# Eight of 24 chunk systems inverted whole on VectorE, and a later due time for K and Q loads

## The chip, the cores and the metric

One NeuronCore of a Trainium2 chip runs the whole program. The metric is the device time of one execution in microseconds; the time quoted is the median of the timed runs. Engines are named as in the profile: PE is TensorE (PEld its weight loads), DVE is VectorE, ACT is ScalarE, POOL is GpSimd, SP issues the DMAs.

## What is computed

A delta-rule attention layer (4 batches, 8 heads, 768 tokens, head size 48), followed by two feed-forward layers with 384 inputs and 2048 hidden units, all in float32.

```python
def _attn_ref(q, k, v, beta):
    k_n = k / (np.linalg.norm(k, axis=-1, keepdims=True) + 1e-06)
    state = np.zeros((B, H, D, D)); y = np.zeros_like(q)
    for t in range(S):
        kt, vt, bt = (k_n[:, :, t], v[:, :, t], beta[:, :, t, None])
        y[:, :, t] = np.einsum('bhd,bhde->bhe', q[:, :, t], state)
        v_old = np.einsum('bhde,bhd->bhe', state, kt)
        state = state + bt[:, :, :, None] * np.einsum('bhd,bhe->bhde', kt, vt - v_old)

h = x @ w_in;  g = np.maximum(h, 0.0) + np.log1p(np.exp(-np.abs(h)));  x = g @ w_out
h = x @ w2_in; g = h * np.cos(h);                                      out = g @ w2_out
```

## The kernel before

The 768 tokens are cut into 24 chunks of 32 (`C`), four chunks to a group (`NG` = 6 groups). Within a chunk the recurrence is a 32 x 32 unit lower triangular system for each batch and head. The kernel inverts its two 16 x 16 diagonal blocks ahead of time and couples them with matmuls in the step. All matmuls run on float16 pairs: a value is split in a high and a low part (`copy`, then a subtraction by `tt` or `stt`), and a product takes three passes (`HI_FIRST`), of which one pass over eight heads is eight matmuls of 48 columns.

The work of a group is in four parts:

- `norms(g)`: loads K of four chunks (`kt`), squares them on ScalarE into `sq`, reduces, takes reciprocal norms. For every group but the first it runs during the steps of the group before.
- `prep_k`, `prep_q`, `gram`: K is scaled, split, transposed, Q is loaded (`qt`) and split, both are stored (`kqd`) and loaded again as block-diagonal operands (`bdK`, `bdQ`, `bdA`); 40 matmuls of 64 columns give the gram of a chunk in `psA`. `take_A` copies its two diagonal blocks into `abuf` by an ACT copy and a DVE combination (with mask columns), and writes the coupling block `G` as a pair into the tail of `kp`; `take_P` makes the masked Q part; one DMA stores all of it (`kpd`).
- `solve(g)`: four chunks at once. DVE transposes `abuf` into `mlan`, so that each partition holds one system; it multiplies by beta and runs 15 pairs of multiply (`tmpd`) and subtract (`tlan`) for both blocks together. The result is split (`t16`), transposed into `tg`, stored in `tgd`.
- `step(n)`: `bt` from the state (matmuls with `bdK`), split to `b16`; a product with T (`bdT`, or `bdU`, which lies in the memory of `raw`) gives `u`; `u16` times the coupling block `bdG` corrects `bt`; split again; T product again; `u16` again; then the state, the output `y` and its transposed store to `xt`.

The first feed-forward layer runs in 12 blocks of two chunks (`moe_block(0, j)`: matmuls `psH<-xt,w` and `acc<-g,w` of 256 columns), the second in six blocks of 512 columns (`psH`, `psC`, `psY<-xu,v`). Weights are loaded as 64-bit words and converted on DVE, ACT and POOL (`conv`, tile `cv`). The second layer's weights take the memory of the whole preparation, which `open_wp2` frees after the last solve.

No order of the instructions is written by hand. `Plan` collects all operations with costs and dependences by keys, lays them out by a list schedule (six passes, priorities from a backward pass), and each engine then runs its queue in that order. A DMA counts as landed 0.9 us plus its `dma` and `slack` times after its issue; `slack` moves the users of a load later in the order, and the load earlier.

Of the kernel before, what the change touches and what calls it, by code (L numbers as in the profile page):

```python
# [52 lines left out]
N2 = C // 2  # L53
BOOST = 0.95
# [231 lines left out]
def delta_moe_moe_kernel(ctx, tc, q, k, v, beta, mask, w1, w2, out):  # L286
# [15 lines left out]
    mask_sb = const.tile([P, C + 3], F32, name="mask_sb")  # L302
# [36 lines left out]
    kpf = [pre.tile([P, 56 * C], F16, name=f"kp{i}") for i in range(4)]  # L339
    kpb = [x[:, 0:48 * C].rearrange("p (s h d l) -> p s h d l", s=3, h=H, l=2) for x in kpf]  # L340
    kgb = [x[:, 48 * C:].rearrange("p (h t l) -> p h t l", h=H, l=2) for x in kpf]
    kab = [pre.tile([P, H // 2, C, 2], F16, name=f"ka{i}") for i in range(2)]
    kqb = [pre.tile([P, 2, Z], F16, name=f"kq{i}") for i in range(4)]
# [3 lines left out]
    abuf = pre.tile([P, N2, 32], F32, name="abuf")  # L347
    mlan = pre.tile([P, N2, C], F32, name="mlan")
    tlan = pre.tile([P, N2, 2, N2], F32, name="tlan")
    t16 = pre.tile([P, C, C, 2], F16, name="t16")  # L350
    sq = pre.tile([P, H, D], F32, name="sq")
# [19 lines left out]
    kpd = dr.tile([NS, P, C * 56], F16, name="kpd")  # L371
    tgd = dr.tile([NG, P, 4, C * 16], F16, name="tgd")
    x2d = dr.tile([NB2, P, 2 * KC, 4 * P], F16, name="x2d")
# [105 lines left out]
    def norms(g):  # L479
        ss, n0, rn = nrm  # L480
        NK = [("n0",)]
        for n in range(4 * g, 4 * g + 4):
# [3 lines left out]
            dma(kt, k[n].rearrange("p (h d) -> p h d", h=H), kk, [("pre",)], 0.55, **A)  # L486
            if g:
                sqv, qk = sq, ("sq",)
# [3 lines left out]
            actf(sqv, kt, AF.Square, [qk], kk + [("pre",)], DM, **A)  # L492
# [43 lines left out]
    def prep_q(n):  # L536
# [3 lines left out]
        dma(qt, q[n].rearrange("p (s h t) -> p s h t", s=2, h=H), qk, [("pre",)], 0.73, **A)  # L540
        qv = kq[:, 1, 0:32 * C].rearrange("p (s h t l) -> p s h t l", s=2, t=C, l=2)
# [38 lines left out]
    def gram(n, bd, key, parts):  # L580
# [4 lines left out]
        mv = k_rows(n).unsqueeze(1) if n < 4 and s1 == 1 else kqb[s][:, s0:s1]  # L585
# [458 lines left out]
```

## Time and profile before

| | us |
|---|---|
| timed runs, median of 3 (lowest, highest) | 1045.03 (1044.27 to 1048.64) |
| profiled execution, its own time | 1038.81 |
| its span from first to last instruction | 1037.0 |
| TensorE busy | 940.1 (91%) |
| VectorE busy | 664.3 (64%) |
| ScalarE busy | 675.5 (65%) |
| mean granted clock of TensorE | 0.985 of full |

Busy time is a mean over stages: about 100 us of preparation and first steps, then 24 steps beside the first layer's blocks until about 660 us, then the second layer alone. Idle time of an engine is worth reading only where something behind it waits.

### The profile page before, as it was taken

Reading aid. Unit: us, or ns where it says so; the run is one execution under the profiler, and the core shown is the slowest. Engines: PE = TensorE matmul, PEld = TensorE weight load, DVE = VectorE, ACT = ScalarE, POOL = GpSimd, SP = SyncE. Lnnn points to the kernel's source line nnn. Section 1 sums busy time; section 2 is a strip of 40 time slices with the busy share of each in tenths; the row PEclk is TensorE's granted clock in tenths of the full one; section 3 lists DMA queues with packets and bytes.
Section 4 is the critical chain, followed back from the end, with each engine's and each line's share of the span. In section 5 each row is a group of like instructions: output and inputs, shape, how many; then the busy total and the mean of one; then the engine's idle time right before and its main releaser. Section 6 shows DMA issues by size and latency. Waiting matters only on the chain.

```text
span 1037.0 us, 27821 instructions
## 1 busy us (share of the span) xinstructions
PE 940.1 (91%) x11552; PEld 685.6 (66%) x11552; DVE 664.3 (64%) x1189; ACT 675.5 (65%) x1273; POOL 364.9 (35%) x331
## 2 busy tenths in 40 slices
PE   1135989989999999999999999999999999999998
PEld 1134878878898899899999997744444444444443
DVE  8999967457746854863575665686555555455454
ACT  5355858676777776866767887865555555554554
POOL 4012436333423442432332545553332223233232
PEclk9998989989999999999999999999999999999999
DMA  6998786877767775674558862101001010000000
GB/s 198 282 265 203 157 210 136 178 178 153 195 84 174 158 160 111 136 160 72 118 120 207 243 147 83 47 32 61 31 1 61 1 61 1 31 31 1 31 1 31
DMA packets 307741, 117.94 MB, mean 114 GB/s; under 512 B 272160, under 2 KB 287648, under 8 KB 307616
## 3 DMA queue, kind: packets, MB, share of 16 engines
q1 hardware_dynamic: 307616, 116.17, 46.4%
q8 instruction: 91, 1.49, 0.6%
q14 instruction: 34, 0.28, 0.1%
HBM read 71.03 MB, written 35.65 MB: 103 GB/s over the span
## 4 chain that ended last, share of the span: by engine, by line
PE 68%; DVE 11%; DMA 7%; ACT 7%; SPq 4%; issue 3%; POOL 1%; DVEq 0%; POOLq 0%; ACTq 0%
PE psH L812 19%; PE accA L874 14%; PE accB L874 10%; PE psC L812 7%; PE psA L874 6%; PE psC L691 5%; PE psY L812 4%; SPq L380 4%; PE psY L691 2%; DMA kt<-k_dram 2%; DMA kpd<-kp 2%; DMA qt<-q_dram 2%; DVE tmpd L401 1%; PE psA L597 1%; DVE cv L458 1%
## 5 line engine op out<-in xcount | busy, mean ns | idle before, releaser
L401 POOL TENSOR_TENSOR g<-g,g 128x512 f16<-128x512 f32 x191 | 227.4, 1191 | 464.9 <-ACT g L389 453.1
L812 PE MATMUL psH<-xt,w 128*128 128x256 f16 x1728 | 231.4, 275 | 3.3 <-DMA xt<-y 2.2
L389 ACT ACTIVATE g<-g 128x512 f16<-128x512 f32 x192 | 120.6, 629 | 100.2 <-DVE g L405 70.3
L874 PEld LDWEIGHTS <-w 128*128 128x128 f16 x1728 | 162.8, 98 | 24.8 <-issue 5.3
L812 PEld LDWEIGHTS <-w 128*128 128x128 f16 x1728 | 157.7, 98 | 22.1 <-DMA xt<-y 2.3
L874 PE MATMUL accA<-g,w 128*128 128x256 f16 x1152 | 159.9, 276 | 4.2 <-ACT g L389 2.8
L874 PEld LDWEIGHTS <-v 128*128 128x128 f16 x864 | 84.6, 98 | 101.9
L812 PEld LDWEIGHTS <-v 128*128 128x128 f16 x864 | 84.6, 98 | 100.9
L410 ACT ACTIVATE e<-e 128x512 f32<-128x512 f32 x96 | 60.4, 629 | 82.1 <-DVE e L405 82.0
L401 DVE TENSOR_TENSOR g<-psH,e 128x512 f32<-128x512 f32 x96 | 66.1, 688 | 55.9 <-ACT e L412 48.0
L874 PE MATMUL accB<-g,w 128*128 128x256 f16 x576 | 94.6, 273 | 0.3 <-POOL g L401 0.2
L812 PE MATMUL psH<-xu,v 128*128 128x512 f16 x351 | 83.1, 379 | 0.0
L812 PE MATMUL psC<-xu,v 128*128 128x512 f16 x342 | 81.5, 379 | 0.0
L874 PE MATMUL accB<-g,v 128*128 128x512 f16 x288 | 77.8, 379 | 0.0
L874 PE MATMUL accA<-g,v 128*128 128x512 f16 x288 | 77.8, 379 | 0.0
L874 PE MATMUL psA<-g,v 128*128 128x512 f16 x288 | 77.7, 379 | 0.0
L691 PEld LDWEIGHTS <-bdKQ 128*128 128x128 f16 x1840 | 65.1, 98 | 12.7 <-issue 10.6
L829 ACT ACTIVATE e<-psH 128x512 f32<-128x512 f32 x96 | 56.6, 590 | 22.6 <-PE psH L812 22.0
L412 ACT ACTIVATE e<-e,hpi 128x512 f32<-128x512 f32 x96 | 69.2, 721 | 3.0
L691 PEld LDWEIGHTS <-bdA 128*128 128x128 f16 x1680 | 56.1, 98 | 15.2 <-issue 13.0
L412 ACT ACTIVATE e<-e 128x512 f32<-128x512 f32 x96 | 60.0, 625 | 1.2
L835 ACT ACTIVATE e<-e 128x512 f32<-128x512 f32 x96 | 59.6, 621 | 0.0
(146 smaller groups left out, 1483.3 us busy)
## 6 DMA issues: line engine op xcount, KB each, us to landing
bdKQ<-kqd SPq DMA_DIRECT2D x184, 64.0 KB, 2.8
kpd<-kp SPq DMA_DIRECT2D x24, 448.0 KB, 3.8
kqd<-kq SPq DMA_DIRECT2D x20, 512.0 KB, 4.6
raw<-w_dram SPq DMA_DIRECT2D x12, 768.0 KB, 4.7
bdA<-kpd SPq DMA_DIRECT2D x96, 96.0 KB, 3.4
w<-w_dram SPq DMA_DIRECT2D x10, 768.0 KB, 6.4
v<-w_dram SPq DMA_DIRECT2D x10, 768.0 KB, 6.5
qt<-q_dram SPq DMA_DIRECT2D x24, 256.0 KB, 4.2
```

Source lines behind the costliest of these rows:

```text
L380: put([("SP", issue)], w, r, lambda e: nc.sync.dma_start(out=dst, in_=src), dma=eng_us, **kw)
L389: nc.scalar.activation(out=out, in_=in_, func=AF.Copy, scale=scale)
L401: put(var, w, r, lambda e: eng[e].tensor_tensor(out=out, in0=a, in1=b, op=op), port=True, **kw)
L410: nc.scalar.activation(out=out, in_=in_, func=func, scale=scale)
L412: nc.scalar.activation(out=out, in_=in_, func=func, scale=scale, bias=bias)
L458: put([("DVE", dve(n))], ck, key, lambda e: nc.vector.scalar_tensor_tensor(cv, in0=half(1), scalar=-0x40000000, in1=cv, op0=ALU.bitwise_an ...
L597: nc.tensor.matmul(ps[:, h], lhsT=w, rhs=x, start=(i == 0), stop=(i == len(ops) - 1))
L691: nc.tensor.matmul(ps[:, h, 0:D], lhsT=lhs(h), rhs=mov[:, h], start=(first and i == 0 and h == 0), stop=(last and i == len(passes) - 1 and ...
L812: nc.tensor.matmul(hp[:, i] if ph == 0 else hp, lhsT=w[:, l, kc * P:(kc + 1) * P], rhs=xv[:, m * KC + kc], start=(kc == 0 and idx == 0), s ...
L829: nc.scalar.activation(out=ev, in_=hv, func=AF.Abs, scale=sc)
L835: put([("ACT", act(n))], ek, [], lambda e: nc.scalar.activation(out=ev, in_=ev, func=AF.Exp, scale=-1.0 if how[0] == "ACT" else -sc))
L874: nc.tensor.matmul(acc[c], lhsT=w[:, l, c * P:(c + 1) * P], rhs=rhs, start=(f == 0 and idx == 0 and (ph == 1 or c != 1)), stop=(f == NF - ...
```

## The change

For chunks 16 to 23 (`n >= NC`) the 32 x 32 inverse is formed whole: `solve` keeps all 32 columns of the gram (`abuf`, `mlan` doubled, for every group), and for groups 4 and 5 it also computes the lower left block in `xlan`, by `below`: 16 multiply-subtract pairs between those of the two diagonal blocks and 15 behind them. The step of these chunks has one T product and no `bdG` product. In chunks 0 to 15 the coupling block gets its own tile (`kG`) and store (`gd`). The squares of `norms` are written into `abuf`. K and Q loads from group 1 on get a `slack` of 3.0. Core of the diff:

```diff
+NC = 16
-    abuf = pre.tile([P, N2, 32], F32, name="abuf")
-    mlan = pre.tile([P, N2, C], F32, name="mlan")
+    abuf = pre.tile([P, C, 32], F32, name="abuf")
+    mlan = pre.tile([P, C, C], F32, name="mlan")
+    xlan = pre.tile([P, N2, N2], F32, name="xlan")
-    sq = pre.tile([P, H, D], F32, name="sq")
+    sq = [abuf.rearrange("p j m -> p (j m)")[:, DM * i:DM * (i + 1)].rearrange("p (h d) -> p h d", h=H) for i in range(2)]
...
-            dma(kt, k[n].rearrange("p (h d) -> p h d", h=H), kk, [("pre",)], 0.55, **A)
+            dma(kt, k[n].rearrange("p (h d) -> p h d", h=H), kk, [("pre",)], 0.55, slack=3.0 if g else 0.0, **A)
-        dma(qt, q[n].rearrange("p (s h t) -> p s h t", s=2, h=H), qk, [("pre",)], 0.73, **A)
+        dma(qt, q[n].rearrange("p (s h t) -> p s h t", s=2, h=H), qk, [("pre",)], 0.73, slack=3.0 if n >= 4 else 0.0, **A)
...
     def take_A(n, ps, pk):
-        copy(av, ps[:, :, 0:N2], mask_sb[:, C + 1:C + 2], [("abuf", i)], r, 128, ps=True, **A)
-        stt(av, ps[:, :, N2:], mask_sb[:, C + 2:C + 3], av, ALU.mult, ALU.add, [("abuf", i)], r, 128, **A)
-        copy(kg[:, :, :, 1], ps[:, :, N2:], 1.0 / K_SC, [("kp", s, 4)], r, 128, ps=True, **A)
+        copy(abuf[:, :, i * 8:i * 8 + 8].rearrange("p j h -> p h j"), ps, 1.0 / (K_SC * K_SC),
+             [("abuf", i)], pk + [("pre",)], 256, ps=True, **A)
+        if n < NC:
+            copy(kg[:, :, :, 1], ps[:, :, N2:], 1.0 / K_SC, [("kG", s, 0)], pk + [("pre",)], 128, ps=True, **A)
...
+            dma(gd[n], kg.rearrange("p h t l -> p (h t l)"), [("gd", n)], [("kG", s, 0), ("kG", s, 1), ("pre",)], 0.2, **A)
...
+        def below(k, c, row, r, w, dst, rd, wr):
+            tv = tmpx[0][:, 0:r * w].rearrange("p (i l) -> p i l", l=w)
+            tt(tv, c.unsqueeze(2).to_broadcast([P, r, w]), row.unsqueeze(1).to_broadcast([P, r, w]), ALU.mult,
+               [("tx", 0)], [("m",)] + rd + PR, r * w, only=on, **A)
+            tt(dst, dst, tv, ALU.subtract, wr, [("tx", 0)] + PR, r * w, only=on, **A)
...
+            if 4 * g + 4 > NC:
+                below(j, m[:, j, N2:], t[:, j, 0, 0:w], N2, w, x[:, :, 0:w], [("td", j)], XR)
+        for j in range(N2 - 1 if 4 * g + 4 > NC else 0):
+            below(j, m[:, N2 + j, N2 + j + 1:], x[:, j], N2 - 1 - j, N2, x[:, j + 1:], [("xr", j)], XR[j + 1:])
...
     def step(n):
-        group(u, ("psC", 1), by_T)
-        take_u()
-        x = ps_c[0]
-        group(x, ("psC", 0), [(lambda h, l=l: col(bdG, h, l), u16[:, m], bk("bdG") + [("u16", m)])
-                              for l, m in HI_FIRST])
...
-        take_b()
-        group(u, ("psC", 1), by_T)
+        if n < NC:
+            take_u()
+            x = ps_c[0]
+            group(x, ("psC", 0), [(lambda h, l=l: col(bdG, h, l), u16[:, m], bk("bdG") + [("u16", m)])
+                                  for l, m in HI_FIRST])
...
+            take_b()
         take_u()
```

VectorE at the step of chunk 20, before: `bt` from the state, first and second half with their splits (`b`, `u`), the first layer's output conversions (`xs`) and the second layer's first weight (`cv`) among them.

```order
L405 SCALAR_TENSOR_TENSOR bt<-psC_145,vt_107 128x384
L405 SCALAR_TENSOR_TENSOR b_110<-bt,b_110 128x384
L405 SCALAR_TENSOR_TENSOR u_111<-psC_146,u_111 128x384
L405 SCALAR_TENSOR_TENSOR xs<-accA,xs 128x512
L405 SCALAR_TENSOR_TENSOR bt<-psC_145,bt 128x384
L405 SCALAR_TENSOR_TENSOR xs<-accB,xs 128x256
L405 SCALAR_TENSOR_TENSOR b_110<-bt,b_110 128x384
L401 TENSOR_TENSOR g_93<-psH_140,e_95 128x512
L456 TENSOR_SCALAR cv_88<-raw_87 128x768
L405 SCALAR_TENSOR_TENSOR u_111<-psC_146,u_111 128x384
```

VectorE at the same step after the change.

```order
L408 SCALAR_TENSOR_TENSOR bt<-psC_148,vt_107 128x384
L404 TENSOR_TENSOR g_93<-psH_143,e_95 128x512
L408 SCALAR_TENSOR_TENSOR b_110<-bt,b_110 128x384
L404 TENSOR_TENSOR g_94<-psH_144,e_96 128x512
L408 SCALAR_TENSOR_TENSOR u_111<-psC_149,u_111 128x384
L459 TENSOR_SCALAR cv_88<-raw_87 128x768
```

One `b` and one `u` are left of two, and the correction of `bt` is gone.

VectorE near the end of the solve for chunks 20 to 23, before: the last pairs, a MoE unit's `g`, the transpose `tg`.

```order
L401 TENSOR_TENSOR tmpd<-mlan,tlan 128x56
L405 SCALAR_TENSOR_TENSOR y_112<-psY,y_112 128x384
L401 TENSOR_TENSOR tlan<-tlan,tmpd 128x2x2x14
L401 TENSOR_TENSOR tmpd<-mlan,tlan 128x30
L401 TENSOR_TENSOR tlan<-tlan,tmpd 128x2x15
L401 TENSOR_TENSOR g_94<-psH_141,e_96 128x512
L662 STREAM_TRANSPOSE tg<-t_136 128x32x32
```

The same place after the change: the end of the diagonal blocks, and the first of the pairs that follow them.

```order
L404 TENSOR_TENSOR tmpd<-mlan,tlan 128x56
L404 TENSOR_TENSOR tx_139<-mlan,tlan 128x224
L404 TENSOR_TENSOR tlan<-tlan,tmpd 128x2x2x14
L404 TENSOR_TENSOR xlan<-xlan,tx_139 128x16x14
L404 TENSOR_TENSOR tmpd<-mlan,tlan 128x30
L404 TENSOR_TENSOR tx_139<-mlan,tlan 128x240
L404 TENSOR_TENSOR tlan<-tlan,tmpd 128x2x15
L404 TENSOR_TENSOR xlan<-xlan,tx_139 128x16x15
L404 TENSOR_TENSOR tx_139<-mlan,tlan 128x256
L404 TENSOR_TENSOR xlan<-xlan,tx_139 128x256
L404 TENSOR_TENSOR g_94<-psH_144,e_96 128x512
L404 TENSOR_TENSOR tx_139<-mlan,xlan 128x240
```

The new pairs (`tx`, `xlan`) stand between the old ones; another 29 of their instructions follow the last row here before `tg`.

ScalarE where the third K load of group 2 is squared (`sq<-kt`), before: `y` and `u` of chunk 2's step, the square, then a MoE unit.

```order
L412 ACTIVATE e_96<-e_96 128x512
L389 ACTIVATE y_112<-psY 128x384
L389 ACTIVATE u_111<-psC_146 128x384
L410 ACTIVATE sq<-kt_115 128x384
L829 ACTIVATE e_95<-psH_140 128x512
L840 ACTIVATE psH_140<-psH_140 128x512
```

The same square (`abuf<-kt`) after the change; `y` of chunk 2 stands 21 rows ahead of it.

```order
L392 ACTIVATE u_111<-psC_149 128x384
L392 ACTIVATE g_97<-g_94 128x512
L867 ACTIVATE e_95<-psH_143 128x512
L878 ACTIVATE psH_143<-psH_143 128x512
L873 ACTIVATE e_95<-e_95 128x512
L413 ACTIVATE abuf<-kt_115 128x384
L392 ACTIVATE b_110<-bt 128x384
L415 ACTIVATE e_95<-e_95 128x512
```

The square has moved behind another MoE unit's instructions; the load itself stands behind chunk 2's transposed store on SP, where it stood ahead of it.

## Rows read from the trace of the kernel before

**Rows 1.** Page: shares by engine, and TensorE's busy tenths in 40 slices
```profile
PE 940.1 (91%) x11552; PEld 685.6 (66%) x11552; DVE 664.3 (64%) x1189; ACT 675.5 (65%) x1273; POOL 364.9 (35%) x331
PE   1135989989999999999999999999999999999998
```

**Rows 2.** Busy time by stretch; the first line names the columns
```profile
core 0: us, PE busy (x) PEld busy (x) DVE busy (x) ACT busy (x) POOL busy (x), PEclk, DMA share, GB/s
26.00:52.00 26.00, 4.14 (x141) 3.88 (x137) 24.16 (x62) 10.44 (x19) 0.52 (x1) 1.00 0.91 284
...
416.00:468.00 52.00, 50.55 (x932) 46.59 (x931) 38.59 (x84) 40.51 (x86) 21.80 (x22) 1.00 0.72 148
468.00:520.00 52.00, 52.00 (x945) 48.19 (x944) 25.58 (x48) 36.01 (x73) 15.17 (x15) 1.00 0.50 95
```

**Rows 3.** TensorE's timeline: start, duration, instruction, count [idle before]
```profile
457.20 0.77 PE L691 MATMUL psC<-b,bdT 128*128 128x48 f16 x24
457.81 1.80 PE L812 MATMUL psH<-xt,w 128*128 128x256 f16 x15
459.44 0.77 PE L691 MATMUL psC<-u,bdG 128*128 128x48 f16 x24
...
545.49 0.77 PE L691 MATMUL psC<-b,bdT 128*128 128x48 f16 x24
```

**Rows 4.** Groups by shape: busy us, mean ns of one, idle before
```profile
L405 DVE SCALAR_TENSOR_TENSOR b<-bt,b 128x384 f16<-128x384 f32 x48 | 31.8, 663 | 21.6 <-ACT b L389 21.5
...
L662 DVE STREAM_TRANSPOSE tg<-t 128x1024 f32<-128x1024 f32 x6 | 11.9, 1991 | 1.8 <-POOL t L401 1.7
...
L405 DVE SCALAR_TENSOR_TENSOR abuf<-psA,mask_sb,abuf 128x128 f32<-128x128 f32 x21 | 9.4, 446 | 7.7 <-ACT abuf L389 7.6
...
L632 DVE STREAM_TRANSPOSE mlan<-abuf 128x512 f32<-128x512 f32 x6 | 4.3, 710 | 0.2
```

**Rows 5.** Timelines of VectorE and GpSimd in the solve for chunks 20 to 23
```profile
516.35 0.71 DVE L632 STREAM_TRANSPOSE mlan<-abuf 128x512 f32<-128x512 f32 x1
...
526.93 0.28 DVE L401 TENSOR_TENSOR tmpd<-mlan,tlan 128x120 f32<-128x120 f32 x1
527.25 0.28 DVE L401 TENSOR_TENSOR tlan<-tlan,tmpd 128x120 f32<-128x120 f32 x1
527.45 0.55 DVE L405 SCALAR_TENSOR_TENSOR u<-psC,u 128x384 f16<-128x384 f32 x1
...
530.12 1.16 POOL L401 TENSOR_TENSOR g<-g,g 128x512 f16<-128x512 f32 x1 [5.35 <-ACT g L389]
530.13 1.22 DVE L401 TENSOR_TENSOR tmpd<-mlan,tlan 128x56 f32<-128x56 f32 x1
...
534.65 2.00 DVE L662 STREAM_TRANSPOSE tg<-t 128x1024 f32<-128x1024 f32 x1 [1.26 <-POOL t L401]
```

**Rows 6.** Who waited for whom, 104:470: us in total, times, longest
```profile
ACT sq L410 <- DMA kt<-k_dram: 9.8, 5, 4.4
```

**Rows 7.** Timelines of SP, ScalarE and TensorE around waits
```profile
127.23 3.95 SPq L380 DMA_DIRECT2D bdKQ<-kqd  x4
131.23 0.96 SPq L380 DMA_DIRECT2D kt<-k_dram  x2
...
134.28 0.52 ACT L410 ACTIVATE sq<-kt 128x384 f32<-128x384 f32 x1 [4.45 <-DMA kt<-k_dram]
...
104.32 0.82 PE L812 MATMUL psH<-xt,w 128*128 128x256 f16 x3 [2.21 <-DMA xt<-y]
...
137.30 0.80 PE L691 MATMUL psC<-b,raw 128*128 128x48 f16 x16 [3.81 <-ACT b L389]
...
189.34 0.56 PE L691 MATMUL psC<-b,raw 128*128 128x48 f16 x16 [1.59 <-ACT b L389]
...
437.45 0.36 PE L691 MATMUL psY<-u,bdA 128*128 128x48 f16 x8 [1.11 <-ACT u L389]
```

**Rows 8.** Busy time by stretch, columns as in rows 2
```profile
136.00:144.00 8.00, 6.70 (x108) 5.79 (x108) 5.63 (x18) 4.28 (x9) 1.16 (x1) 0.58 0.74 175
```

More of the change, by code (lines that the diff above doesn't have):

```diff
@@ L658, in solve @@
[L658 removed]
+        Z = [("t16", "z")]
+        copy(to[1], tv, 1.0, [("t16", 1)], ROW + PR + Z, 512, fast=False, **A)
+        tt(to[0], tv, to[1], ALU.subtract, [("t16", 0)], ROW + PR + [("t16", 1)] + Z, 512, pool_c=1.225, **A)
         tw_ = t16.rearrange("p i l x -> p (i l x)").bitcast(F32).rearrange("p (i l) -> p i l", l=C)
         gw = tg.rearrange("p n h i x -> p (n h i x)").bitcast(F32).rearrange("p (n i) -> p i n", i=C)
[L661 to L662 removed]
@@ L663, in solve, with turn @@
-        if g == 0:
-            for b in range(B):
-                rows = slice(32 * b, 32 * b + 32)
-                copy(bdT[rows, :, b], tg[rows, 0].rearrange("p h i x -> p h (i x)"), 1.0, [("bdT", b)],
-                     [("tg",), ("bdT", "z")] + PR, 512, **A)
-        dma(tgd[g], tg.rearrange("p n h i x -> p n (h i x)"), [("tgd", g)], [("tg",)] + PR, 1.46, **A)
+        def turn(n0, n1):
+            put([("DVE", 1.135)], [("tg",)], [("t16", i) for i in range(4)] + Z + PR,
+                lambda e: nc.vector.transpose(out=gw, in_=tw_), **A)
+            if n0 == 0 and g == 0:
+                for b in range(B):
+                    rows = slice(32 * b, 32 * b + 32)
+                    copy(bdT[rows, :, b], tg[rows, 0].rearrange("p h i x -> p h (i x)"), 1.0, [("bdT", b)],
+                         [("tg",), ("bdT", "z")] + PR, 512, **A)
+                n0 = 1
+            dma(tgd[g, :, n0:n1], tg[:, n0:n1].rearrange("p n h i x -> p n (h i x)"), [("tgd", 4 * g + n) for n in range(n0, n1)],
+                [("tg",)] + PR, 0.37 * (n1 - n0), **A)
@@ new lines, in solve, with load_G @@
+        n0 = min(max(NC - 4 * g, 0), 4)
+        if n0:
+            turn(0, n0)
+        if n0 == 4:
+            return
+        xo = [t16[:, N2:, 0:N2, i] for i in range(2)]
+        copy(xo[1], x, 1.0, [("t16", 3)], XR + PR + Z, 256, fast=False, **A)
+        tt(xo[0], x, xo[1], ALU.subtract, [("t16", 2)], XR + PR + [("t16", 3)] + Z, 256, **A)
+        turn(n0, 4)
+    def load_G(n):
+        src = gd[n].rearrange("p (h x) -> p h x", h=H)
+        for b in range(B):
+            rows = slice(32 * b, 32 * b + N2)
+            dma(bdG[rows, :, b, C:], src[rows], [("bdG", b)], [("gd", n), ("bdG", "z")], 0.11, slack=slack[0], **A)
@@ L674, in load_T @@
     def load_T(n):
-        bd_load(*bd_T(n), tgd[n // 4, :, n % 4], [("tgd", n // 4)], 0.22)
-    def load_G(n):
-        src = kpd[n, :, 48 * C:].rearrange("p (h x) -> p h x", h=H)
-        for b in range(B):
-            rows = slice(32 * b, 32 * b + N2)
-            dma(bdG[rows, :, b, C:], src[rows], [("bdG", b)], [("kpd", n), ("bdG", "z")], 0.11, slack=slack[0], **A)
+        bd_load(*bd_T(n), tgd[n // 4, :, n % 4], [("tgd", n)], 0.22)
     def load_v(n):
```

96 lines of the change are left out of this document (50 added, 46 removed).

## The prediction

> **What bounds the kernel now.** I read the shares and slices of the page first, then busy time by stretch, then TensorE's own timeline, and last who waited for whom. TensorE is busy for 940.1 of 1037.0 us, and its idle time lies almost wholly in front [rows 1]. The stretch table makes this exact: 468:520 has 52.00 of 52.00 us on TensorE, as have the stretches behind it up to the tail, while VectorE has 25.58 there [rows 2]. So work taken off TensorE behind 468 us comes off the end, as long as its queue finds the next instruction ready. Before that, 416:468 is 1.45 us short. The first 104 us are another matter: VectorE is at 24.16 of 26 us and TensorE at 4.14 [rows 2].
>
> The profiled execution took 1038.81 us (span 1037.0); the median of the timed runs is 1045.03, 6.2 more. I sum differences and put them on the median.
>
> **Part 1, removed from TensorE.** Each of chunks 16 to 23 loses one product with T (24 matmuls) and one with the coupling block (24): 8 x 48 = 384 matmuls of 48 columns, of 11552. Their price is read where the queue is full: a group of 24 starts at 457.20 and the next instruction at 457.81 [rows 3]. That is 0.61 us for 24, 25.2 ns each (the 0.77 us shown for the group runs to the end of the last one, which the next overlaps). 384 x 25.2 ns = 9.7 us, all in steps 16 to 23. The first T product of step 16 stands at 457.20, step 20's at 545.49 [rows 3], so this is the full stretch: **-9.7 us**. The ScalarE and VectorE work of the dropped half (two copies and three VectorE instructions a chunk, the longest the rest of b with 0.66 us [rows 4]) shortens the step's chain. I cost it at nothing, because TensorE has other work meanwhile.
>
> **Part 2, added to VectorE.** The solve of each of the last two groups gets 62 more instructions: 16 pairs (multiply, subtract) of 16 x w elements for w = 1 to 16, and 15 pairs of 16 x r for r = 15 to 1. That is 2 x 2176 + 2 x 1920 = 8192 elements. What one costs depends on its neighbour. Alone in its chain, the 120-element subtraction at 527.25 starts 0.32 us behind the one it waits for at 526.93; an instruction that needs nothing of it follows after 0.20 [rows 5]. I split these as 0.19 us + elements/960 in a chain and 0.07 + elements/960 beside other work. The order shows the first 32 new ones woven between the old chain's, so they go at the second price: old and new there are 62 instructions and 7072 elements, 62 x 0.07 + 7.4 = 11.7 us, where the old chain alone took 30 x 0.19 + 2.8 = 8.5. The other 30 are one chain: 30 x 0.19 + 4.0 = 9.7. So the solve grows by 11.7 + 9.7 - 8.5 = 12.9 us. To this come a transpose of 1024 instead of 512 elements (1991 against 710 ns [rows 4]: +1.3), the multiplication by beta doubled (+0.5), and a smaller last conversion (-1.1). Of the 30 old instructions with their chain in group 5, three are stretched, by 0.5 to 1.0 us, each beside a GpSimd instruction (530.13, 1.22 us beside the one from 530.12 [rows 5]): 2.1/30 x 62 = +4.3. Some six more MoE and step instructions stand in between, about +2. Sum: **+20 us a solve**.
>
> Who waits is TensorE, whose order is fixed: step 16's and step 20's first T product. What covers it is the work queued ahead. Counted in the two orders, between the last gram of the group and that product stood 231 matmuls of 256 columns and 256 of 48; now 378 and 440. At 109 ns (15 in 1.63 us [rows 3]) and 25.2 ns this is 19.5 us more cover for group 4, and by 219 to 381 and 256 to 392 it is 21.1 us for group 5. So 20 against 19.5 and 21.1: the T block arrives about when it is asked for. Before, TensorE did not wait at 545.49, and by 1.11 us near the other solve (437.45) [rows 3, 7]. I take **+2 us** for both. Below: 0 (a late block can't gain). Above: if none of the new instructions finds company, the first 32 cost 32 x 0.19 + 4.5 = 10.6 instead of 3.2, +7.4 a solve, about +17 in all.
>
> [...]
>
> **Part 3, K and Q counted as landing 3 us later.** This alters the order alone. In the stretch 104:470 ScalarE waited 9.8 us for K in five places [rows 6], and hardly for Q. The worst: at 131.23 the K load gets out behind four bdKQ loads that held SP for 3.95 us, ScalarE stands idle 4.45 us before its square, and TensorE stops 3.81 us at 137.30 [rows 7]. [...] TensorE's wait at 189.34 (1.59) stands behind a K wait too [rows 7], and one more like it. Sum 3.8 + 2 x 1.6 + 3.4, about 10. The new order has 20 ScalarE instructions between the output copy of that chunk and the square, where it had one; on SP the load has moved too, from four entries ahead of that chunk's transposed store to right behind it. So the square should find its data there. But the squares are now written into the memory of the solve's input, so that the first of a group waits for the solve's long transpose. All other placements are new too. From 104.32 to 457.20 us TensorE worked off 2028 matmuls of 256 columns, 3136 of 48 and 600 of 64, which I take at the price of 48: 315 us in 353 [rows 3, 7]. So 38 us went to waits and the lower clock, most of it behind other loads and engines. A new order draws these again. I take **-4 us**, with ends of -10 and +8.
>
> **Part 4, the start.** VectorE sets it. Up to the second output conversion it had 185 instructions and has 176. Off go five abuf combinations (5 x 0.45 [rows 4]) and some ten that move to ScalarE or behind, on come the longer transpose and multiplication (+1.8) and two weight conversions. Net about -1.5 by rows, but solve 0 itself is 1.8 longer, and a small gd store now stands ahead of the second pair of Q loads on SP, behind a VectorE instruction. I take **0**, with ends of -3 and +4. The other two small changes (kpd stored without its coupling part, 16 gd stores) are hidden beside other transfers: the DMA engines are at 0.72 and 0.50 of their time in 416:520 [rows 2].
>
> Sum: -9.7 + 2 - 4 + 0 = -11.7; 1045.0 - 11.7 = **1033**.
>
> **Rivals.**
> *K and Q waits go wholly, the solves are in time*: -9.7 - 10 and the start's -1.5 = 1024. For it: each of the five waits was under 4.5 us. Chance 0.17.
> *The reordering gives it back*: the matmuls go, but the 38 us of loss between 104 and 457 us comes out 8 us larger by chance placement, or TensorE lacks converted second-phase weights at the end of phase one, since solve 5 opens their memory: -9.7 + 2 + 8, about 1045. For it: 38 us is a large quantity to redraw. Against it: counted in MoE units of VectorE's order, the weight conversions begin within four units of where they did. Chance 0.19.
> *The solve is late, and the kernel slower*: place, the T products of steps 16 and 20; price, TensorE stopped by 8 to 9 us at each if the new instructions run one behind the other, more where GpSimd stretches them (at the 0.5 us excess on one in three: 62/3 x 0.5 = 10 a solve in place of 4.3). 17 + 2 x 5.7 - 9.7 = +19, 1064 at worst; 1054 halfway. It decides from 7.5 us of lateness a solve. Chance 0.09. [...]
> *It doesn't do what it says*: the freed time isn't on the bound. The full stretch behind 468 us speaks against it; the reordering rival contains it.
> Forecast: 0.55.
>
> **How the numbers follow.** The forecast's own range is 1028 to 1040. For 8 in 10 I go down to 1022 (most of the first rival) and up to 1046 (the bulk of the reordering rival); what is left out is the deep end of the first and the late solve. 0.5%, about what a measurement of this kernel can tell, is 1039.8 to 1050.3. Faster: 0.17 + 0.53 of the forecast + 0.04 of the reordering = 0.74. Same: 0.02 + 0.13 of these two + 0.03 of the late solve = 0.18. Slower: 0.02 + 0.06 = 0.08.
>
> **What would show it.** TensorE has 11168 matmuls and no wait behind 470 us; waits at step 16's or 20's T product measure part 2. The distance from the solve's first transpose to its last (20.3 us before in group 5 [rows 5]) should be near 40. ScalarE's 9.8 us on K should fall under 4. The first MoE matmul stays at 104 +- 4 us. If the time falls with K waits unchanged, part 3 is wrong; if TensorE waits at steps 16 and 20 for more than 3 us each, part 2 is.

## The result and the profile after

The changed kernel took 1057.67 us (median of 4 runs, 1054.35 to 1060.30), the kernel before on the same chip 1044.65. The ratio is 1.0127 with a 95% interval of 1.0094 to 1.0161: 13 us slower, where 12 us faster was forecast. The profiled execution took 1056.73 us with a span of 1054.5.

The page of the changed kernel: busy time by engine, then TensorE's busy tenths over 40 slices of the span.

```profile
PE 935.3 (89%) x11168; PEld 678.0 (64%) x11168; DVE 687.7 (65%) x1255; ACT 671.7 (64%) x1253; POOL 364.0 (35%) x335
PE   1135879789899998989998899999999999999998
```

The 384 matmuls are gone (11168 against 11552 in [rows 1]). But TensorE is idle for 119 us of its span, against 97 before, and two of its slices behind the middle (some 554 to 606 us) show 8s, where the kernel before had nines [rows 1]. Its busy time fell by 4.8 us only, for matmuls that the prediction prices at 9.7; the mean granted clock of this execution is 0.953, against 0.985 before.

Half of the added idle time shows in three stretches, beside the two long solves and behind the second. First the kernel before, then the changed one (columns: length, busy time and instructions of PE, PEld, DVE, ACT, POOL; granted clock; DMA share; GB/s).

```profile
442.00:468.00 26.00, 25.66 (x438) 23.54 (x435) 17.16 (x32) 18.91 (x38) 10.27 (x10) 1.00 0.79 164
546.00:572.00 26.00, 26.00 (x499) 24.12 (x495) 16.55 (x27) 20.70 (x40) 7.43 (x7) 1.00 0.86 225
572.00:624.00 52.00, 52.00 (x837) 47.74 (x833) 34.62 (x49) 43.41 (x80) 26.05 (x18) 1.00 0.72 185
```

```profile
442.00:468.00 26.00, 24.22 (x300) 21.48 (x299) 25.11 (x64) 17.80 (x34) 10.20 (x10) 1.00 0.16 28
546.00:572.00 26.00, 23.76 (x288) 21.17 (x286) 19.61 (x43) 17.93 (x34) 8.33 (x9) 1.00 0.23 55
572.00:624.00 52.00, 44.51 (x740) 40.11 (x737) 29.03 (x41) 34.15 (x63) 18.24 (x14) 0.97 0.93 213
```

Read the DMA share first. While each solve runs, the DMA engines go nearly idle (0.16 and 0.23, before 0.79 and 0.86), and right behind the second they are crowded (0.93), and TensorE idles for 7.5 us there. The count of matmuls says the same: 300 and 288 where 438 and 499 stood. TensorE is busy with MoE matmuls of 256 columns, and the attention chain with its 48-column ones nearly stands still: 24 matmuls of `psC` in 451:469, where the kernel before has 152. The loss behind the second solve is another matter: e9, below, has it without a long solve. SyncE's queue in the changed kernel (start, length, operation, number merged) and its longest wait between 436 and 472 (total, times, longest):

```profile
449.16 2.63 SPq L383 DMA_DIRECT2D bdA<-kpd  x4
469.08 0.36 SPq L383 DMA_DIRECT2D tgd<-tg  x1
...
541.57 2.63 SPq L383 DMA_DIRECT2D bdA<-kpd  x4
562.57 0.36 SPq L383 DMA_DIRECT2D tgd<-tg  x1
...
596.73 8.06 SPq L383 DMA_DIRECT2D bdA<-kpd  x4
```

```profile
SPq L383 <- DVE st L408: 17.6, 1, 17.6
```

SyncE issues nothing from 451.8 to 469.1 and from 544.2 to 562.6: the next entry of its queue is the store of the finished T blocks. (The wait row names the VectorE instruction `st`, which starts at 468.88; the store reads `tg`, whose transpose runs from 467.02 to 469.04.) In the kernel before, sixteen rows of that list start between 442 and 469. And TensorE in the changed kernel:

```profile
207.88 2.31 PE L604 MATMUL psA<-kq,bdA 128*128 128x64 f16 x40 [6.31 <-DMA bdA<-kq]
...
478.20 0.77 PE L730 MATMUL psC<-b,bdT 128*128 128x48 f16 x24
...
571.65 0.77 PE L730 MATMUL psC<-b,bdT 128*128 128x48 f16 x24
...
607.28 0.80 PE L730 MATMUL psY<-u,bdA 128*128 128x48 f16 x16 [4.57 <-DMA bdA<-kpd]
```

The T products of steps 16 and 20 have no wait before them, but stand at 478.20 and 571.65 where they stood at 457.20 and 545.49 [rows 3]: 21.0 and 26.2 us later. The largest idle piece behind 468 us is the wait of 4.57 us for a bdA load at 607.28, which is one of the four whose issue took 8.06 us (2.63 for the like four at 541.57). The largest between 104 and 468 is a gram that waited 6.31 us for its bdA load, at 207.88.

### The profile page after: what moved, and what is told of

Read it like the earlier page. It is cut to its first block, busy times and chain, and to the rows that moved or that the text cites. A ratio compares the mean times of both kernels' runs of the same rounds, so it can differ in the third digit from the quotient of the medians.

```text
span 1054.5 us, 27098 instructions
## 1 busy us (share of the span) xinstructions
PE 935.3 (89%) x11168; PEld 678.0 (64%) x11168; DVE 687.7 (65%) x1255; ACT 671.7 (64%) x1253; POOL 364.0 (35%) x335
## 4 chain that ended last, share of the span: by engine, by line
PE 63%; DVE 11%; DMA 9%; SPq 6%; ACT 5%; issue 3%; POOL 1%; DVEq 0%; ACTq 0%; POOLq 0%
PE psH L850 17%; PE accA L912 12%; PE accB L912 9%; PE psC L850 7%; PE psA L912 6%; SPq L383 5%; PE psC L730 5%; PE psY L850 3%; PE psY L730 2%; DMA qt<-q_dram 2%; PE psA L604 2%; DMA bdA<-kq 2%; DMA kqd<-kq 2%; DVE tx L404 1%; DVE cv L461 1%
## 5 line engine op out<-in xcount | busy, mean ns | idle before, releaser
L850 PE MATMUL psH<-xt,w 128*128 128x256 f16 x1728 | 226.6, 275 | 3.6 <-DVE g L404 3.5
L912 PEld LDWEIGHTS <-w 128*128 128x128 f16 x1728 | 163.8, 98 | 20.1
L850 PEld LDWEIGHTS <-w 128*128 128x128 f16 x1728 | 161.0, 98 | 23.5 <-issue 4.3
L912 PE MATMUL accA<-g,w 128*128 128x256 f16 x1152 | 157.3, 275 | 0.0
L413 ACT ACTIVATE e<-e 128x512 f32<-128x512 f32 x96 | 60.4, 629 | 84.0 <-DVE e L408 84.0
L912 PE MATMUL accB<-g,w 128*128 128x256 f16 x576 | 91.9, 275 | 0.0
L730 PEld LDWEIGHTS <-bdKQ 128*128 128x128 f16 x1840 | 61.6, 98 | 13.0 <-issue 11.2
L415 ACT ACTIVATE e<-e 128x512 f32<-128x512 f32 x96 | 60.0, 625 | 1.3
L408 DVE SCALAR_TENSOR_TENSOR g<-psC,e 128x512 f32<-128x512 f32 x38 | 26.3, 692 | 53.0 <-ACT e L415 51.4
```

Source lines behind the costliest of these rows:

```text
L408: lambda e: nc.vector.scalar_tensor_tensor(out, in0=a, scalar=s, in1=b, op0=op0, op1=op1), port=True, **kw)
L413: nc.scalar.activation(out=out, in_=in_, func=func, scale=scale)
L415: nc.scalar.activation(out=out, in_=in_, func=func, scale=scale, bias=bias)
L730: nc.tensor.matmul(ps[:, h, 0:D], lhsT=lhs(h), rhs=mov[:, h], start=(first and i == 0 and h == 0), stop=(last and i == len(passes) - 1 and ...
L850: nc.tensor.matmul(hp[:, i] if ph == 0 else hp, lhsT=w[:, l, kc * P:(kc + 1) * P], rhs=xv[:, m * KC + kc], start=(kc == 0 and idx == 0), s ...
L912: nc.tensor.matmul(acc[c], lhsT=w[:, l, c * P:(c + 1) * P], rhs=rhs, start=(f == 0 and idx == 0 and (ph == 1 or c != 1)), stop=(f == NF - ...
```

## The experiments

Each time is a median, each ratio is to the kernel before on the same chip, with its 95% interval.

**Is it the K and Q slack?** e1 puts the slack alone into the kernel before, e2 takes it out of the changed one, e4 is the kernel before with a slack of 0.25, which only makes the ordering pass choose another order.

```diff
-dma(kt, k[n]..., kk, [("pre",)], 0.55, **A)
+dma(kt, k[n]..., kk, [("pre",)], 0.55, slack=3.0 if g else 0.0, **A)     # and Q; e4: 0.25; e2: 0.0
```

> The kernel before with the 3 us on the K and Q loads alone; 11552 matmuls as before, short solves. Three theories. Late Q (the slack itself does harm: the K loads land in time, the Q loads and the gram loads behind them then do not): at least half of the changed kernel's 8.9 us of extra TensorE idle time between 104 and 468 us is here, time 1050 to 1055 us, ScalarE waits over 8 us for Q. Long solve (the loss lies in the solves behind 416 us, the slack is harmless): 1035 to 1046, TensorE stays full behind 468 us. Scatter (each order is a new draw of the same work): anything from 1036 to 1056, with waits at other places than in the changed kernel.

> The changed kernel without the slack on K and Q; 11168 matmuls, long solves in the last two groups. Late Q: the loss ahead of 468 us goes, ScalarE's 13 us for Q fall under 4, time 1036 to 1046. Long solve: TensorE still idles by 10 us or more behind 468 us, and the second-phase weight loads still begin near 572 us instead of 546; time 1048 to 1056. Scatter: no direction, 1040 to 1060.

> The kernel before with 0.25 us on the K and Q loads in place of 3: the same instructions, and a landing time that hardly differs, so the ordering pass has no better or worse knowledge, only another draw. Scatter: the time moves by 3 us or more to either side of 1045, with TensorE waits at other places. Late Q and long solve, where orders of equal knowledge cost the same: 1043 to 1048, within 0.3% of the kernel before.

e1: 1041.91, 0.9996 (0.9970 to 1.0022). e2: 1056.73, 1.0122 (1.0075 to 1.0170). e4: 1044.37, 0.9998 (0.9976 to 1.0020). The slack neither does harm nor gains by itself, and the "late Q" theory falls. e4 also bears on the scatter theory: the same work in another order had other waits, and came out within 0.1%.

**Is it the long solve?** e3 sets NC = 24: every chunk keeps its coupling product, no solve is long, the rest of the change stays. e12 has only the last group's solve long.

```diff
-NC = 16
+NC = 24        # e12: 20
```

> The changed kernel with the coupling product kept for all 24 chunks (NC = 24): the new stores and loads, the 32-row abuf transpose and the slack stay, the 62 instructions a solve go, the 384 matmuls come back (11552). Long solve: TensorE is full behind 468 us again (under 3 us idle between 468 and 624), and the time is 1045 to 1052, the loss ahead of 468 alone. Late Q: the same waits for Q ahead of 468, 1050 to 1056. Scatter: 1040 to 1062 with waits at new places.

> The changed kernel with NC = 20: only the last group's solve is long, 11360 matmuls. Long solve, one half of it: idle time of TensorE behind 468 between those of NC = 24 (6.8 us) and of the changed kernel (13.5), second-phase weights still late (near 570), 1050 to 1056. If the loss came from group 4's solve alone (VectorE crowded in 420 to 468, K chain of group 5 behind it): under 7 us idle behind 468 and 1042 to 1049.

e3: 1053.24, 1.0110 (1.0070 to 1.0150). e12: 1058.77, 1.0143 (1.0109 to 1.0177). So with no long solve and with all matmuls back the kernel is still 11 us slower than before: something else in the change costs. And with one long solve the kernel is no faster than with two, though e12 also keeps 192 of the matmuls (4.8 us at the prediction's price); e12 lies above both its ranges, and e3 above the range of the long solve.

**The tie of the squares.** In the changed kernel the squares of K are written into abuf, so those of the next group must wait until a solve has read it. e5 adds that tie, and nothing else, to the kernel before. e6 takes it out of the changed one (squares into the chunk's own kq buffer, so that they wait for the users of that buffer instead). e7 gives the coupling rows four buffers instead of two, e8 does both.

```diff
 # e5, in the kernel before
-actf(sqv, kt, AF.Square, [qk], kk ...
+actf(sqv, kt, AF.Square, [qk] + ([("abuf", s % 2), ("abuf", 2 + s % 2)] if g else []), kk ...
 # e6, in the changed kernel
-sqv, qk = sq[s % 2], ("abuf", s % 2)
+sqv, qk = sq[s], ("kq", s, 0)
 # e7
-            s = n % 2
+            s = n % 4
             kg = kgb[s]
```

> The kernel before, instruction for instruction, with one thing added: the squares of a group's K count as writing the solve's input abuf (and their sums as reading it), as in the changed kernel, so that they may not start before the solve of the group ahead has transposed it. No slack, short solves, 11552 matmuls. Theory of the tie (squares of group g+1 held until solve g reads abuf, their sums placed at the solve's end, and with them the whole K chain of the next group): 1050 to 1058 us, squares in pairs right behind a solve's first transpose and at its end, TensorE idle over 25 us between 104 and 468. Rival (the tie is harmless, the loss comes from the gd stores with two kG buffers, or from the longer transposes): 1041 to 1048, as e1 and e4.

> The changed kernel with the tie taken away: the squares are written into the K part of the chunk's own kq buffer, which is free when the gram of the group ahead has been loaded, instead of into abuf. The rest stays: slack, gd stores, long solves, 11168 matmuls. Theory of the tie: the loss of 13 us and the 10 us of matmuls both come back, 1033 to 1042, second-phase weight loads near 550 us. If the long solve holds the rest back: TensorE still idles over 6 us behind 468, 1044 to 1050. If the two kG buffers are to blame: 1052 to 1058, as before the edit.

> The changed kernel with four kG buffers in place of two (two of them in the memory of the inverse's lower half, which is free until group 4); the tie stays. Theory of the tie: 1053 to 1059, within 0.4% of the changed kernel, though ScalarE's 9.0 us for the gd stores go. Rival (kG): 1042 to 1050.

> Both edits in the changed kernel: squares in kq, four kG buffers. Theory of the tie: as the one with the squares alone, within 5 us, 1030 to 1042. Rival (kG): well below the one with the squares alone, by 6 us or more.

e5: 1037.08, 0.9945 (0.9922 to 0.9968). e6: 1062.44, 1.0205 (1.0156 to 1.0254). e7: 1061.70, 1.0196 (1.0146 to 1.0245). e8: 1063.49, 1.0211 (1.0168 to 1.0254). My theory of the tie fell, and with the opposite sign: the tie makes the kernel before faster, and putting another tie in its place makes the changed one slower; e5 lies below both its ranges, e6 above all of its own. Four buffers did not help either: e7 lies above both its ranges.

**The order or the work?** Three kernels separate the 62 instructions a solve from the order that is made around them. In e9 they are neither planned nor issued; in e10 they are planned with their full cost, so that the order on every engine is that of the changed kernel, but none is issued; in e11 they are issued, but planned at 1 ns. The T blocks of e9 and e10 lack the lower half of the last eight chunks.

```diff
 def below(k, c, row, r, w, dst, rd, wr):
+    return                                                # e9
...
+    put([("DVE", dve(r * w))], ..., lambda e: None, ...)  # e10: counted, not issued
+    put([("DVE", 1e-3)], ..., tensor_tensor, ...)         # e11: issued, not counted
```

> The changed kernel without the 62 VectorE instructions of the lower half in each of the last two solves; they are left out of the ordering pass too, and the T blocks lack that half. 11168 matmuls, all else as in the changed kernel, order drawn anew. Theory of the long solve (its 20 us on the way to the T block push the attention chain of the last groups back, and with it the second-phase memory): TensorE is full behind 468 us again (under 3 us idle), weight loads of the second phase begin near 546, and the 9.7 us of matmuls come off: 1030 to 1040. Rival (the loss lies in the other edits: stores of the coupling rows, 32-row transposes, ScalarE's larger copies): 1046 to 1056, TensorE idles over 8 us behind 468.

> The changed kernel in its own order on every engine: the ordering pass counts the 62 instructions a solve, but none is issued (the T blocks lack the lower half). So only VectorE's time for them goes. If their execution holds TensorE up (VectorE busy beside the MoE units, late T blocks, late second-phase weights): TensorE's idle time behind 416 falls by 8 us or more, time 1044 to 1049. If the order made around them is to blame: within 4 us of the changed kernel, 1053 to 1058, with waits at the same places.

> The changed kernel with the 62 instructions a solve issued, but counted at next to nothing (1 ns each) in the ordering pass. So the order is made as if the solve were short, and TensorE meets the T products of steps 16 and 20 some 20 us early. If the order made around the long solve is to blame: this is no worse than the changed kernel, 1045 to 1058, with waits at the T products of steps 16 and 20. If the execution of the solve is what costs: TensorE stops by 10 to 18 us at each of the two T products, 1060 to 1075.

e9: 1041.87, 0.9990 (0.9969 to 1.0012). e10: 1055.00, 1.0106 (1.0054 to 1.0157). e11: 1068.63, 1.0243 (1.0214 to 1.0273). This is the clearest answer of the study: without a single one of the new instructions, the order of the changed kernel still takes 1055. And it is that order: in the two traces every engine runs the same instructions in the same sequence, all 11168 matmuls and 770 DMA issues, apart from the 62 a solve. VectorE in e10, where the second long solve would be:

```profile
543.59 0.69 DVE L404 TENSOR_TENSOR g<-psH,e 128x512 f32<-128x512 f32 x1 [1.70 <-ACT e L415]
548.27 0.69 DVE L404 TENSOR_TENSOR g<-psH,e 128x512 f32<-128x512 f32 x1 [3.99 <-POOL g L404]
...
551.68 0.69 DVE L404 TENSOR_TENSOR g<-psH,e 128x512 f32<-128x512 f32 x1 [2.25 <-ACT e L415]
555.61 0.69 DVE L404 TENSOR_TENSOR g<-psH,e 128x512 f32<-128x512 f32 x1 [3.25 <-ACT e L415]
...
560.70 1.99 DVE L688 STREAM_TRANSPOSE tg<-t 128x1024 f32<-128x1024 f32 x1 [3.93 <-POOL t L404]
```

and SyncE and TensorE of e10:

```profile
544.71 1.32 SPq L383 DMA_DIRECT2D bdA<-kpd  x2
562.71 0.36 SPq L383 DMA_DIRECT2D tgd<-tg  x1
```

```profile
478.11 0.77 PE L729 MATMUL psC<-b,bdT 128*128 128x48 f16 x24
```

VectorE now has nothing to compute for the solve and idles, but the transpose that ends it comes at 560.70, as in the changed kernel (560.55). Its queue is worked off in the plan's order, and between the solve's parts stand MoE multiplications, which in 540:563 waited 7.2 us for ScalarE's `e` and 4.0 us for GpSimd's `g`; the transpose waited 3.9 us for GpSimd's `t`. So a solve that the plan believes long is late even when it costs nothing: SyncE again issues nothing for 16.7 us, and step 16's T product stands at 478.11. In e9 it stands at 464.28, and the store of the T blocks goes out at 455.05 (468.54 in e10):

```profile
464.28 0.77 PE L731 MATMUL psC<-b,bdT 128*128 128x48 f16 x24
```

```profile
455.05 0.35 SPq L383 DMA_DIRECT2D tgd<-tg  x1
```

e9 lies between its two ranges, and does not fit the theory of the long solve in full: TensorE idles for 8.2 us behind 468 in it, where under 3 were expected. Against the changed kernel it shows what the long solve takes from TensorE, and what it does not. First two stretches and a wait of e9, then the first stretch of the changed kernel:

```profile
416.00:572.00 156.00, 154.80 (x2641) 142.23 (x2639) 97.02 (x190) 116.54 (x235) 58.60 (x59) 1.00 0.67 140
572.00:624.00 52.00, 44.97 (x661) 39.90 (x660) 28.12 (x39) 37.04 (x66) 20.92 (x15) 0.93 0.78 204
```

```profile
614.92 1.12 PE L731 MATMUL psY<-u,bdA 128*128 128x48 f16 x24 [4.76 <-DMA bdA<-kpd]
```

```profile
416.00:572.00 156.00, 147.17 (x2379) 133.34 (x2378) 120.10 (x299) 109.65 (x219) 56.87 (x57) 1.00 0.55 114
```

Beside and between the solves, in 416:572, the changed kernel idles for 7.6 us more than e9. But in 572:624 e9 idles for 7.0 us, the changed kernel for 7.5, and the wait for bdA is there in e9 too, though its first second-phase weight load goes out at 551.98. So the crowding behind step 20 is not the long solve's doing; the kernel before and e18 idle there for 0.1 us at most, and which of the other edits brings it stays open.

In e11 I expected TensorE to stop at the T products. It does not: step 16's comes at 486.97 without a wait. The longest wait between 420 us and it is in the MoE units, whose VectorE multiplication stands behind the solve. The time was as expected, the place was not. e11 is also 26 us behind e9, though its order is not quite e9's either: as far as one order shows, a long solve without room costs more than the room that the plan makes for it.

```profile
472.28 1.44 PE L852 MATMUL psH<-xt,w 128*128 128x256 f16 x6 [3.47 <-DVE g L404]
```

**The separate store of the coupling rows.** e13 puts kG, gd and its store and loads into the kernel before; e14 takes them out of e3 (rows back in kp and kpd).

```diff
 # e13, in the kernel before (e14: the reverse, in e3)
-kg = kgb[s]
+kg = kgb[n % 2]
...
+dma(gd[n], kg.rearrange("p h t l -> p (h t l)"), [("gd", n)], [("kG", n % 2, 0), ("kG", n % 2, 1), ("pre",)], 0.2, **A)
...
-src = kpd[n, :, 48 * C:].rearrange("p (h x) -> p h x", h=H)
+src = gd[n].rearrange("p (h x) -> p h x", h=H)
```

> The kernel before with one edit of the change: the coupling rows go to two kG buffers and get a store of their own (24 small stores more on SyncE's queue), the kp store is shorter. No slack, short solves, 11552 matmuls, 16-row transposes. If the separate store is what costs in the NC = 24 kernel: 1049 to 1056, with TensorE's grams waiting for bdA by 8 us or more in 104 to 468. If it is one of the other edits: 1037 to 1046.

> The NC = 24 kernel (e3, 1053.2) with the coupling rows back in kp and its store, as before the change; transposes of 32 rows, squares in abuf and the slack stay. If the separate store costs: 1037 to 1045. If one of the other edits: 1049 to 1056.

e13: 1051.65, 1.0090 (1.0066 to 1.0114). e14: 1048.35, 1.0070 (1.0046 to 1.0095). The store (24 of them here, 16 in the changed kernel), with its two buffers, costs the kernel before 9 us; taking it out of e3 gives 4 back, which the intervals do not tell from nothing. e14 stays 7 us above the kernel before, between its two ranges, so the store is one of at least two causes. In e13, ScalarE's waits for transfers and TensorE's waits for ScalarE's copies in 104:470 (us in total, times, longest):

```profile
ACT kp L389 <- DMA kpd<-kp: 25.7, 11, 4.6
ACT sq L410 <- DMA kt<-k_dram: 16.6, 6, 7.6
ACT kq L389 <- DMA qt<-q_dram: 8.5, 4, 3.3
ACT kG L389 <- DMA gd<-kG: 2.7, 1, 2.7
```

```profile
PE psC L692 <- ACT b L389: 17.7, 7, 5.5
PE psY L692 <- ACT u L389: 9.9, 4, 5.4
```

Only 2.7 us is a wait for the new store itself. In the kernel before the first three were 17.6, 9.8 [rows 6] and 1.2, and the last two 6.0 and 5.3. ScalarE waits for these three for 22 us longer, and the attention chain's small copies (b, u), which stand behind them on the same queue, make TensorE wait 16 us longer (in e17, below, 5 and 9 us longer). That the one wait is handed on as the other is read from the queue's order; no run shows how much of it is. The gram waits for bdA that the expectation named are hardly there (1.8 us).

**Chance or not?** Each cost above rests on one order. e15 and e16 draw e9 and e10 again, e17 and e18 draw e13 and e5 again, by the K and Q slack, which by itself does nothing.

```diff
-slack=3.0 if g else 0.0      # e9, e10
+slack=0.0 if g else 0.0      # e15, e16; and for Q. e17, e18: e13 and e5 with 3.0
```

> e9 (the 62 instructions a solve neither planned nor issued, 1041.9) with the K and Q slack at zero: another draw of the order for the same work. A steady cost of planning the long solve: 1038 to 1046 again. Chance: anywhere up to 1056. Leaves out the lower half of the T blocks of the last eight chunks.

> e10 (planned, but not issued, 1055.0) with the K and Q slack at zero: another draw. A steady cost: 1051 to 1059 again, 10 us or more above e15, with the T product of step 16 near 478 us and the second-phase weight loads near 570. Chance: within 5 us of e15. Leaves out the lower half of the T blocks of the last eight chunks.

> The kernel before with the separate store of the coupling rows (e13, 1051.65), and the 3 us of slack on K and Q as a new draw. The store costs steadily: 1047 to 1055. Chance of the draw: 1037 to 1046, like e1 and e4.

> The kernel before with the squares tied to the solve ahead (e5, 1037.1), and the 3 us of slack as a new draw. The tie gains steadily: 1033 to 1040. Chance of the draw: 1041 to 1050.

e15: 1048.30, 1.0059 (1.0027 to 1.0092). e16: 1055.79, 1.0124 (1.0084 to 1.0164). e17: 1053.06, 1.0064 (1.0035 to 1.0092). e18: 1039.09, 0.9921 (0.9895 to 0.9947). e15 lies above its 1046. The planned solve costs again, though 7 us, not the 10 or more expected, since e15 is the one redraw that moved much (by 7 us; the other five pairs with and without slack differ by at most 2.7). Step 16's T product stands at 484.23 in e16 and at 464.96 in e15, and e16 and e2 again have the same order on every engine. The store and the tie repeat. e18, the kernel before with the tie and the slack, is the fastest kernel of the study, 8 us ahead of the kernel before and clear of the changed one.

**A path from the kernel before to the changed one.** Taken in this order, seven runs lead from one to the other, by one edit or one group of edits at a time. Shares are of 1044 us. By the intervals of the two ratios, an estimate, each difference is good to some 2 to 6 us; the slack, the first figure of the store and the last row can't be told from nothing.

| step | run | ratio | this edit | on a second pair |
|---|---|---|---|---|
| squares tied to the solve ahead | e5 | 0.9945 | -5.7 us | -7.8 (e1 to e18), -8.1 (e6 to changed, another tie) |
| slack on K and Q | e18 | 0.9921 | -2.5 | -0.4 (before to e1), -2.7 (e13 to e17), +0.5 (e2 to changed) |
| solve on 32 rows, and the rest of the layout | e14 | 1.0070 | +15.6 | none |
| separate store of the coupling rows | e3 | 1.0110 | +4.2 | +9.4 (before to e13), +7.1 (e1 to e17) |
| 384 matmuls and their copies go, with 8 stores and 32 loads of coupling rows | e9 | 0.9990 | -12.5 | none |
| 62 instructions a solve, planned | e10 | 1.0106 | +12.1 | +6.8 (e15 to e16) |
| the same, issued | changed | 1.0127 | +2.2 | -0.2 (e16 to e2) |

The stretches 104:468 and 468:728 along this path (columns as above), in the order before, e18, e14, e9, e10, changed:

```profile
104.00:468.00 364.00, 342.69 (x6000) 310.53 (x6001) 243.92 (x506) 267.45 (x574) 143.94 (x149) 0.97 0.72 156
468.00:728.00 260.00, 260.00 (x3332) 207.10 (x3331) 164.41 (x260) 193.00 (x345) 109.25 (x82) 1.00 0.46 114
```

```profile
104.00:468.00 364.00, 343.33 (x6063) 314.02 (x6061) 247.76 (x510) 268.05 (x576) 144.63 (x148) 0.97 0.69 151
468.00:728.00 260.00, 259.41 (x3328) 205.72 (x3327) 165.72 (x266) 193.12 (x344) 104.61 (x81) 1.00 0.49 125
```

```profile
104.00:468.00 364.00, 338.92 (x5935) 309.29 (x5936) 234.29 (x486) 263.67 (x562) 143.94 (x145) 0.96 0.69 149
468.00:728.00 260.00, 254.46 (x3353) 205.37 (x3350) 166.62 (x258) 190.22 (x344) 101.11 (x80) 0.99 0.52 120
```

```profile
104.00:468.00 364.00, 339.60 (x5864) 308.44 (x5862) 232.61 (x472) 261.64 (x551) 136.25 (x140) 0.97 0.68 146
468.00:728.00 260.00, 251.77 (x3051) 198.72 (x3049) 161.12 (x245) 188.55 (x336) 106.41 (x87) 0.99 0.52 124
```

```profile
104.00:468.00 364.00, 334.06 (x5719) 302.37 (x5719) 224.63 (x454) 252.40 (x528) 128.78 (x133) 0.96 0.66 143
468.00:728.00 260.00, 248.91 (x3155) 201.59 (x3152) 162.78 (x250) 189.76 (x347) 111.56 (x92) 0.99 0.54 126
```

```profile
104.00:468.00 364.00, 333.82 (x5743) 302.38 (x5743) 241.13 (x516) 253.81 (x531) 131.21 (x133) 0.96 0.66 143
468.00:728.00 260.00, 246.52 (x3125) 199.63 (x3125) 180.51 (x312) 189.34 (x345) 111.80 (x93) 0.99 0.53 126
```

The idle time (length less the first busy column) is 21.3 + 0 before, 20.7 + 0.6 in e18, 25.1 + 5.5 in e14, 24.4 + 8.2 in e9, 29.9 + 11.1 in e10 and 30.2 + 13.5 in the changed kernel. So the stretch ahead of 468 us loses in two steps, at e14 (4.4 us) and at e10 (5.5). The full stretch behind it is lost bit by bit from e14 on: 4.9 us with the layout, 2.7 up to e9, 2.9 with the plan of the long solve, 2.4 with its instructions.

## Why the prediction was wrong, point by point

*What bounds the kernel.* Right for the kernel before, and the argument's weak link. "Work taken off TensorE behind 468 us comes off the end" held on condition that its queue finds the next instruction ready. I took that condition from a profile in which it held, and the change itself broke it: 13.5 us idle there instead of none, 5.5 of them already in e14, without any long solve.

*Part 1, -9.7.* Right, as far as shown. From e3 to e9 12.5 us went, good to about 5. The two differ by the dropped half of the steps, but also by eight of the small stores, 32 loads of coupling rows and the conversion of the lower half of T, so the price of the matmuls alone is not measured.

*Part 2, +2: one of the two steps that failed.* Its mechanics were right. From its first transpose to its last the solve took 44.2 us in group 4 (422.82 to 467.02) and 40.4 in group 5 (520.12 to 560.55), near the forecast 40; its price by elements, elements/960, fits the trace of before, where in the chain 30 elements took 0.23 us from start to start (531.98 to 532.21) and 128 took 0.33 (525.62 to 525.95); TensorE did not wait at either T product; and with the same order on every engine the instructions themselves cost 2.2 us by e10 to changed, and nothing by e16 to e2, neither told from noise. What failed is the sentence that the 19.5 and 21.1 us of work queued ahead are cover. That work was not free: it was moved from behind the T product to ahead of it. The T products came 21 and 26 us later (14 and 20 of it against e9), the attention steps and their loads nearly stood still meanwhile, and the last T product came at 628.5 instead of 615.4. The second-phase weights followed, with their first load at 572.15 (545.66 before, 551.98 in e9), since their memory opens when the last solve ends. With its order the solve costs 12.1 + 2.2 us, or 6.6 on the second pair, where I had 2. In idle time of TensorE it is 5.8 us ahead of 468 and 5.3 behind, e9 to changed, 7.6 of the two between 416 and 572. Why work moved ahead is not made up for behind is not taken further apart by any run.

*Part 3, -4 with ends of -10 and +8.* The K waits went, as forecast: 9.8 us [rows 6] came down to 1.3. Others took their place, Q first. ScalarE in 104:470 of the changed kernel:

```profile
ACT kq L392 <- DMA qt<-q_dram: 13.1, 4, 6.1
ACT kG L392 <- DMA gd<-kG: 9.0, 2, 6.1
...
ACT abuf L413 <- DMA kt<-k_dram: 1.3, 1, 1.3
```

No run shows the 3.4 us for a lower clock in its sum of about 10 as time lost: the granted clock was 0.58 over 136:144 [rows 8], and over 104:468 it was 0.97 before and 0.96 in the changed kernel, so it did not rise. By itself the slack gave 0.4 us (e1), which can't be told from nothing. That the squares' tie could only cost was wrong: it gained 6 to 8 us in two pairs, and against another tie in a third. Why is open.

*Part 4, 0.* Right. The first MoE matmul stands at 104.98.

*Hidden at no cost: the second step that failed.* I called the 16 small stores of the coupling rows hidden, by the DMA engines' share of 0.72 and 0.50 [rows 2]. The separate store, 24 of it, cost 4 to 9 us in three pairs, two of them clear of noise, and only 2.7 us of ScalarE's time in e13 is a wait for it: with it in the order, ScalarE's queue waits longer for other transfers (by 22 us in e13, 5 in e17). What the 16 of the changed kernel cost was not measured. And I gave the 32-row solve no cost behind the start, because its direct price is about 1 us a solve (the first transpose takes 1.23 us, 0.71 before [rows 4], and not the 1.99 that I took). From e18 to e14 it, together with the other edits of the layout (the squares' true place in abuf, ScalarE's copy of 256 columns, the packed kq), costs 15.6 us. That is the largest step of the path, and the runs do not split it, so which of these edits I priced wrongly at nothing stays open. Nor was it drawn twice, though it is more than twice what any redraw moved.

*The rivals.* "The reordering gives it back" came nearest: idle time ahead of 468 grew by 8.9 us, where it said 8. The loss that it named behind 468, a lack of converted second-phase weights, is not among TensorE's waits there (bdA loads 5.6 us, `st` 4.5, the MoE's `g` 2.2), and it called the cause chance. Six pairs that differ by the slack alone moved by 0.4 to 7 us, the planned solve and the store cost each time. "The solve is late" had the sign and the size, but its place, waits at the T products, stayed empty in the changed kernel and even in e11.

## What to carry to other kernels

When a planner sets the order, the price of a longer step on a side chain can be neither its busy time nor the wait of its consumer, but what the plan moves to make room (here 12.1 and 6.8 us in two pairs, against 2.2 and -0.2 for the instructions themselves): look for the stretch in which the DMA share and the count of the consumer's instructions fall (here from 0.79 to 0.16, and from 438 to 300). To split the two, plan the added instructions without issuing them. Before blaming the step for a loss behind it, look whether the loss is there without the step: the crowded stretch was. And take the "small" edits of a change one at a time: here the small store and the layout edits, the wider input of the solve among them, cost more together (15.6 + 4.2 us) than went with the saved matmuls (12.5).

## What was not expected of the hardware

An instruction of 48 elements on VectorE took 1.05 us in the middle of the long chain, where its like took 0.20 to 0.21. It ended with a GpSimd instruction that ran beside it (first VectorE, then GpSimd, of the changed kernel):

```profile
462.88 0.23 DVE L404 TENSOR_TENSOR xlan<-xlan,tx 128x64 f32<-128x64 f32 x1
463.14 1.05 DVE L404 TENSOR_TENSOR tx<-mlan,xlan 128x48 f32<-128x48 f32 x1
464.22 0.21 DVE L404 TENSOR_TENSOR xlan<-xlan,tx 128x48 f32<-128x48 f32 x1
```

```profile
462.91 1.22 POOL L404 TENSOR_TENSOR g<-g,g 128x512 f16<-128x512 f32 x1 [2.06 <-ACT g L392]
```

Only the second instruction is stretched here; the first ran 0.2 us into GpSimd's at its usual speed. The prediction had counted on such stretches, at 4.3 us a solve: in this solve six of the 62 took 1.05 to 1.33 us, some 5 us more than their like. Also, the issue of four like loads (bdA) took SyncE 2.63 us at 449.16, in a stretch whose DMA share is 0.16, and at 541.57, but 8.06 at 596.73, in a stretch whose share is 0.93; the next entry of its queue went out at 604.84. Another four of that second stretch took 4.10 us at 580.54, and four of the kernel before 8.94 us at 582.68, in the same stretch with a share of 0.72. So that the crowded DMA engines make the issue slow is not shown, only that the slow issues stand in such stretches.
